# A weight ring of seven buffers instead of six, one weight block fewer resident, and two loads of a step issued at other points of it

## The chip, the cores and the metric

The kernel runs on one core of one Trainium2 chip. The metric is the device time of that core in microseconds, from the first to the last instruction, as the median of several runs; the profile is one more execution, with its own, slightly longer span. The engines are called by their short names: PE is TensorE (matmuls; PEld its weight loads), DVE is VectorE, ACT is ScalarE, POOL is GpSimd, and SP is SyncE, which here only issues transfers.

## The reference

Two branches work on the same input x (2048 rows of 640, bf16) and are mixed row by row with a gate.

```python
# branch A: attention over a sliding window of 256, 32 heads of 20
qkv = x @ wqkv
scores = (q @ k^T) * 20 ** -0.5, masked to 0 <= i - j < 256
a = (softmax(scores) @ v) @ wo

# branch B: 64 segments of 32 rows, one after the other, 32 heads of 192, memory of 8 rows
mem = mem0
for s in range(64):
    h = concat(mem, x[32 * s : 32 * s + 32])          # 40 rows of 640
    q, k, v = h @ Wq, h @ Wk, h @ Wv                  # each to 32 x 192
    scores = (q @ k^T) * 192 ** -0.5                  # rows of the memory see all, others causal
    o = (softmax(scores) @ v) @ Wo                    # back to 40 rows of 640
    mem, out[s] = o[:8], o[8:]

g = sigmoid(sum(x * gate_w))
out = g * a + (1 - g) * b
```

Each step of branch B needs the memory rows that the step before made, so the 64 steps run in order, and each needs all of Wq, Wk, Wv and Wo (4 x 640 x 6144 elements, 31.5 MB in bf16)[...].

## The kernel before

**Stages.** First branch A runs block by block (128 rows each) and writes its gated result to DRAM. Then a "tail" stage works ahead for branch B: the last 8 rows of every segment are multiplied with Wq, Wk and Wv for all segments at once, and the products are stored to the DRAM tensor `xin`, one record for each segment. Then come the 64 steps of branch B. Beside the earlier stages the resident weights are loaded.

**Weights.** Each of the four weights is cut into four groups of heads (g) and each group into tiles (m): five for q, k and v (384 KB each), six for o (320 KB each), 84 blocks in all. The table `STREAMED` (L1079) names for each weight and group the tiles that are not kept: 22 of 84. These are loaded again in every step through a ring, the pool `b_w` with `RING` buffers (L1074), by SP, in the order in which PE uses them. The others are resident: `EARLY` of them (L1075) are loaded during branch A, the rest later. A ring block may be issued when the buffer's last user, a matmul `RING` blocks earlier, is done. In the trace the streamed blocks are `b_w`, the resident ones `w_q`, `w_k`, `w_v`, `w_o` and `hold`, the tail stage's ring blocks `w_ring`.

**One step.** `pe_order` (L630) and the string `STEP` (L636) fix PE's order by hand: `k0 q0 k1 tk0 tq0 q1 s0 tk1 q2 tq1 k2 v0 p0 s1 tq2 q3 k3 pv0 tk2 v1 p1 s2 oa0 ...`. Here q, k, v are projections of a group (L796, five tiles each), tq and tk transposes (L820), s scores (L876), p the transposed probabilities (L930), pv the values (L958 and L965), oa and ob the output projection (L991), m the memory rows for the next step (L1014). The other engines' orders come from a planner, `Sched`: each operation is given an engine, a duration, a latency, the buffers it reads and writes, and operations it must follow (`after`); the planner runs them against a model of the engines and takes on each engine the ready one with the longest chain behind it. PE and SP keep their given orders.

**The loads of a step on POOL.** `tail_qk` (L734) loads 48 KB of stored q and k products for each group (`b_xg`). `load_tail` (L727) loads the 96 KB of stored v products of the step (`b_xv`, one buffer), which the second half of each values operation reads (L965). `load_x` (L720) loads the next segment's 40 KB of x (`b_hT`, two buffers). POOL also stores the step's result (L1027), reads branch A's rows (L1028) and stores the mix (L1037), and copies the tail products into place for the scores (L833, L852, L854). In the kernel before, `load_tail(s)` and `load_x(s + 1)` are entered when the first name of step s comes up (L1046), with no operation that they must follow: they may go as soon as their buffer is free.

**Branch A's first block.** In `branch_A` the load of the second block of x (L106) is issued behind that of the value weights (L105). In the loop over blocks (L323) the score units are interleaved with "fill": projections and other work for neighbouring blocks, handed out in proportion to the units done (L345). For the first block, which has four units, all of the fill is handed out by the last unit; after it comes the last masking (`cut`) and then the values (L297).

## Time and profile before

| | |
|---|---|
| time, median of 3 runs | 2000.54 us (2000.38 to 2003.24) |
| span of the profiled execution | 2011.8 us |
| granted PE clock, mean | 0.997 |
| step of branch B, mean of 63 | 24.66 us (23.6 to 26.7) |
| bytes moved in all | 618.98 MB |
| of these by SP's queue (weights, mostly) | 563.31 MB |
| blocks streamed in a step | 15 of 384 KB and 7 of 320 KB |

A page of the profile gives busy time by engine, the chain of waits that set the end, and the costliest groups of instructions. A group's line holds the line of the source, the engine, the operation, the tiles written and read, the count, busy time and mean duration, and the idle time before it with what ended it. The view of stretches gives for a window the busy time of each engine with its number of instructions, the granted clock, the mean busy share of the core's 16 DMA engines, and the bytes moved per time; the share can pass 1 a little because consecutive packets overlap. A transfer's landing time runs from its issue to the last of its completions.

### The profile page before, as it was taken

What the parts mean: (1) busy time and instruction counts of PE and PEld (TensorE: products, weight loads), DVE (VectorE), ACT (ScalarE), POOL (GpSimd) and SP (SyncE); (2) the same over time, 40 slices, a digit from 0 to 9 for tenths busy, and PEclk for the clock granted to TensorE, in tenths of its full rate; (3) what the DMA queues carried; (4) which work ended last, traced back from release to release, by engine and by line L of the source; (5) the groups of instructions that cost most, each with busy time, mean ns of one, the idle gap of its engine ahead of it and who ended that gap; (6) DMA issues with size and microseconds to landing.
All of it is one profiled execution on the core that took longest, in us unless ns stands there. A gap on an engine that the chain in (4) does not pass through costs nothing.

```text
span 2011.8 us, 92168 instructions
## 1 busy us (share of the span) xinstructions
PE 1901.9 (95%) x39590; PEld 1400.1 (70%) x39590; DVE 1012.7 (50%) x3338; ACT 950.0 (47%) x1951; POOL 721.9 (36%) x2015
## 2 busy tenths in 40 slices
PE   8999999989999999999999999999999999999998
PEld 6888878656666666666666666676666666666665
DVE  5777853334454444444444445444444444444444
ACT  4888832334444444444444444444444444444443
POOL 5111121243344333334333334333333433333332
PEclk9999999999999999999999999999999999999999
DMA  4222159789999999999999999999999999999997
GB/s 156 79 81 80 36 149 325 213 286 350 364 358 359 346 352 355 355 350 355 352 355 355 351 360 366 345 361 353 354 352 351 356 352 349 358 353 356 351 351 278
DMA packets 259632, 618.98 MB, mean 308 GB/s; under 512 B 40552, under 2 KB 59408, under 8 KB 259216
## 3 DMA queue, kind: packets, MB, share of 16 engines
q1 hardware_dynamic: 227264, 563.31, 77.4%
q0 software_dynamic: 31952, 49.71, 8.4%
q8 instruction: 312, 5.11, 1.0%
q14 instruction: 104, 0.85, 0.1%
HBM read 583.49 MB, written 29.37 MB: 305 GB/s over the span
## 4 chain that ended last, share of the span: by engine, by line
PE 71%; DMA 21%; DVE 3%; ACT 2%; issue 2%; POOL 0%; ACTq 0%; POOLq 0%; DVEq 0%
PE ps_o L991 17%; PE ps_v L796 9%; PE ps_k L796 9%; PE ps_q L796 8%; DMA b_w<-in_B_Wq_dram 7%; DMA b_w<-in_B_Wv_dram 5%; DMA b_w<-in_B_Wo_dram 5%; PE t_psum L605 5%; DMA b_w<-in_B_Wk_dram 3%; PE t_psv L623 3%; PE S_ps L876 2%; PE qk_ps L155 2%; PE ps_pv L958 2%; PE tr_q L820 2%; PE tr_k L820 2%; PE s_ps L251 2%
## 5 line engine op out<-in xcount | busy, mean ns | idle before, releaser
L796 PEld LDWEIGHTS <-b_hT 128*32 128x32 bf16 x15360 | 372.3, 96 | 251.2 <-issue 52.7
L991 PEld LDWEIGHTS <-b_OT 128*64 128x64 bf16 x6144 | 364.2, 110 | 40.9 <-issue 14.9
L796 PE MATMUL ps_k<-w_k,b_hT 128*32 128x384 bf16 x4352 | 234.1, 327 | 3.8 <-issue 0.7
L991 PE MATMUL ps_o<-hold,b_OT 128*64 128x320 bf16 x2560 | 236.0, 301 | 0.9 <-issue 0.9
L942 DVE TENSOR_TENSOR b_PTm<-PT_ps,marks 128x320 bf16<-128x320 f32 x256 | 125.9, 492 | 195.2 <-PE PT_ps L930 195.2
L796 PE MATMUL ps_q<-w_q,b_hT 128*32 128x384 bf16 x3584 | 223.4, 327 | 0.1
L847 DVE TENSOR_TENSOR b_Kz<-tr_k,marks 128x256 bf16<-128x256 bf16 x256 | 108.2, 423 | 215.3 <-PE tr_k L820 210.1
L796 PE MATMUL ps_v<-w_v,b_hT 128*32 128x384 bf16 x3584 | 213.7, 328 | 2.1 <-issue 2.0
L991 PE MATMUL ps_o<-b_w,b_OT 128*64 128x320 bf16 x1792 | 205.5, 300 | 8.2 <-DMA b_w<-in_B_Wo_dram 7.2
L254 ACT ACTIVATE pt<-s_ps 128x1024 bf16<-128x1024 f32 x180 | 183.3, 1026 | 47.8 <-PE s_ps L251 46.2
L969 ACT CAST b_OT<-ps_pv 128x480 bf16<-128x480 f32 x256 | 143.1, 559 | 129.0 <-PE ps_pv L965 129.0
L807 ACT CAST b_tok<-ps_k 128x384 bf16<-128x384 f32 x256 | 122.7, 479 | 166.6 <-PE ps_k L796 158.4
L807 ACT CAST b_vtok<-ps_v 128x384 bf16<-128x384 f32 x256 | 122.7, 479 | 134.5 <-PE ps_v L796 133.7
L739 POOL DMA_DIRECT2D b_xg<-xin x256 | 141.8, 554 | 88.7 <-POOL b_QT L833 53.0
L991 PE MATMUL ps_o<-w_o,b_OT 128*64 128x320 bf16 x1792 | 170.0, 300 | 0.8 <-issue 0.8
L807 ACT CAST b_tok<-ps_q 128x384 bf16<-128x384 f32 x256 | 122.9, 480 | 95.5 <-PE ps_q L796 94.5
L829 ACT COPY b_QT<-tr_q 128x384 bf16<-128x384 bf16 x256 | 123.3, 482 | 86.2 <-PE tr_q L820 84.2
L852 POOL COPY b_K<-b_xg 128x64 bf16<-128x64 bf16 x256 | 60.7, 237 | 264.1 <-PE S_ps L876 254.0
L1037 POOL DMA_DIRECT2D out_dram<-b_ga x126 | 62.5, 496 | 243.3 <-DVE b_ga L1032 233.8
L1020 DVE CAST b_hT<-mem_ps 128x16 bf16<-128x16 f32 x126 | 22.5, 179 | 247.4 <-PE mem_ps L1014 244.1
L796 PE MATMUL ps_q<-b_w,b_hT 128*32 128x384 bf16 x1536 | 130.3, 329 | 12.2 <-DMA b_w<-in_B_Wq_dram 11.1
L796 PE MATMUL ps_v<-b_w,b_hT 128*32 128x384 bf16 x1536 | 130.7, 328 | 10.5 <-DMA b_w<-in_B_Wv_dram 9.1
(155 smaller groups left out, 3699.2 us busy)
## 6 DMA issues: line engine op xcount, KB each, us to landing
b_w<-in_B_Wq_dram SPq DMA_DIRECT2D x384, 384.0 KB, 5.7
b_w<-in_B_Wv_dram SPq DMA_DIRECT2D x384, 384.0 KB, 5.3
b_w<-in_B_Wo_dram SPq DMA_DIRECT2D x448, 320.0 KB, 5.4
b_w<-in_B_Wk_dram SPq DMA_DIRECT2D x192, 384.0 KB, 5.3
xin<-hold POOLq DMA_DIRECT2D x8, 1536.0 KB, 12.4
b_xg<-xin POOLq DMA_DIRECT2D x256, 48.0 KB, 5.0
w_k<-in_B_Wk_dram SPq DMA_DIRECT2D x17, 384.0 KB, 3.7
b_xv<-xin POOLq DMA_DIRECT2D x64, 96.0 KB, 5.2
```

What stands on the lines that cost most here:

```text
L254: nc.scalar.activation(out=pt, in_=sp[:], func=ACT.Exp, scale=scale)
L605: self.nc.tensor.matmul(pt[:, bb, :], lhsT=w[kt][:, c:c + P], rhs=self.xTb[:, kt, t0:t0 + hs * MEM], start=(kt == 0), stop=(kt == KT - 1))
L739: sc.op("POOL", 540, 5000, lambda: nc.gpsimd.dma_start(tile_of(b)[:].rearrange("p i b t -> p (i b t)"), xin[s, :, c:c + 192]), writes=[b])
L796: nc.tensor.matmul(t[32 * j:32 * j + 32, 0:384], lhsT=tile_of(hT)[:, kt, :], rhs=w[:, j * 384:(j + 1) * 384], start=(kt == 0), stop=(kt == ...
L807: nc.scalar.copy(dst, src)
L820: nc.tensor.transpose(t[64 * a:64 * a + 64, k, :], tok["tile"][:, c:c + 64], ident[:], tile_position=(0, 64 * a))
L829: nc.scalar.copy(dst, tq["tile"][:].rearrange("p b (j t) -> p b j t", t=SEG))
L847: nc.vector.tensor_tensor(out=tile_of(Kz)[:, :, :, 0:SEG], in0=src, in1=mk_z.unsqueeze(1).unsqueeze(3).to_broadcast([P, 4, 2, SEG]), op=AL ...
L942: nc.vector.tensor_tensor(out=tile_of(PTm)[:], in0=src.to_broadcast([P, 2, 4, L]), in1=mk_m.unsqueeze(1).unsqueeze(3).to_broadcast([P, 2, ...
L969: sc.op("ACT", 560, 50, lambda: nc.scalar.copy(tile_of(OT)[:, 0:12 * L], o["tile"][:, 0:12 * L]), reads=[o], writes=[OT])
L991: nc.tensor.matmul(t[64 * h:64 * h + 64, 0:D // 2], lhsT=OT["tile"][:, c:c + 64], rhs=w, start=(g == 0 and m == 0 and n == 0), stop=(g == ...
L1037: sc.op(eng, 500, 3000, lambda h=h: queue.dma_start(half(outf, h), mine(tile_of(ga), h)), reads=[ga])
```

## The change

It has four parts.

- The ring has seven buffers instead of six. One more block is streamed in each step, tile 2 of group 2 of k, and with it 23 of 84 are; one fewer is loaded early (23 instead of 24), so that the space in SBUF stays the same.
- `load_tail(s)` is entered when the first scores operation (s0) of step s comes up, and must follow the operation entered just before, which is ACT's evacuation of q1.
- `load_x(s + 1)` is entered when the first p0 of step s comes up, and must follow ACT's evacuation of v0.
- In branch A the second block of x is loaded ahead of the value weights; and for the first block the fill is handed out more slowly, with the remainder after the last masking and ahead of the values.

```diff
@@ branch_A
             add_qk(1, KT - 1)
+            load_x(1)
             nc.sync.dma_start(wv_sb[:, :, 0:D], wq3[:, :, 2 * D:3 * D])
-            load_x(1)
...
-                while fill and spent * total < (i + 1) * time:
+                while fill and spent * (total + 2 * (nk == 1)) < (i + 1) * time:
                     w, f = fill.pop(0)
...
                 if cut is not None:
                     cut()
                     cut = None
+                for _, f in fill:
+                    f()
                 for r in ready:
@@ branch_B
-    def load_x(s):
+    def load_x(s, after=()):
...
-        return hb, sc.op("POOL", 540, 5000, f, writes=[hb])
+        return hb, sc.op("POOL", 540, 5000, f, writes=[hb], after=after)
-    def load_tail(s):
+    def load_tail(s, after=()):
...
-        if s not in tails:
-            tails[s] = load_tail(s)
-            if s + 1 < nseg:
-                hts[s + 1] = load_x(s + 1)
+        if n[0] == "s" and s not in tails:
+            tails[s] = load_tail(s, [sc.ops[-1]])
+        if n[0] == "p" and s + 1 < nseg and s + 1 not in hts:
+            hts[s + 1] = load_x(s + 1, [sc.ops[-1]])
@@ the tables
-RING = 6
-EARLY = 24
+RING = 7
+EARLY = 23
...
-            "k": ((1,), (4,), (), (4,)),
+            "k": ((1,), (4,), (2,), (4,)),
```

## The prediction

> **What bounds the kernel now.** I read the chain of waits first, then the busy tenths and the transfers, then stretches of the trace. The page gives the span and the chain by engine:

> ```profile
> span 2011.8 us, 92168 instructions
> PE 71%; DMA 21%; DVE 3%; ACT 2%; issue 2%; POOL 0%; ACTq 0%; POOLq 0%; DVEq 0%
> ```

> The end is set by TensorE with weight transfers threaded in; DVE, ACT and POOL (50%, 47%, 36% busy) are nowhere on it for long. The 64 recurrent steps take most of it: the memory matmuls of L1014 first start at 451.1 and last at about 2004.4 us, so 63 step periods of 24.66 us. Three stretches, with the columns PE, PEld, DVE, ACT, POOL busy, clock, DMA share, GB/s: an early one with resident loads alone, the steps, and two moments inside one step:

> ```profile
> 302.00:308.00 6.00, 6.00 (x58) 5.37 (x56) 1.88 (x6) 1.94 (x6) 2.29 (x2) 1.00 1.03 404
> 452.00:2004.00 1552.00, 1471.04 (x33128) 1055.17 (x33120) 746.13 (x2707) 695.39 (x1575) 602.45 (x1753) 1.00 0.98 353
> 996.00:1001.00 5.00, 5.00 (x130) 2.99 (x126) 2.81 (x10) 2.91 (x7) 2.09 (x7) 1.00 1.03 403
> 1004.00:1007.00 3.00, 3.00 (x81) 2.05 (x75) 2.12 (x9) 1.81 (x5) 1.76 (x5) 1.00 0.91 303
> ```

> The reader is to see that a DMA share of 0.98 isn't a full DMA: the same engines move 404 GB/s with a deep queue, 353 on average in the steps, and swing between 403 and 303 inside one step. Why the queue isn't deep shows in issue-to-landing times (minimum, median, maximum): first single resident loads of the k weights between 50 and 220 us, with nothing beside them; then the burst of resident v loads (285 to 330 us); then the ring's blocks:

> ```profile
> DMA to landing us min/median/max: 3.0/3.1/4.3
> ...
> DMA to landing us min/median/max: 9.2/12.0/14.7
> ...
> DMA to landing us min/median/max: 3.6/5.5/11.8
> ```

> SyncE's own waits are mostly for TensorE to give a ring buffer back (the longest of them first), and after them TensorE's waits, in the steps only (us, times, longest):

> ```profile
> SPq L538 <- PE ps_q L796: 224.6, 312, 1.3
> ```

> ```profile
> PE mem_ps L1014 <- ACT b_OT L1000: 35.6, 62, 0.6
> PE ps_q L796 <- DMA b_w<-in_B_Wq_dram: 10.9, 20, 1.4
> PE ps_o L991 <- DMA b_w<-in_B_Wo_dram: 7.0, 12, 1.3
> ```

> With 22 blocks in 24.66 us and 5.5 us to land, 22 x 5.5 / 24.66 = 4.9 of the six buffers are in flight and 1.1 hold data that is waited on or read. So TensorE and the ring drive each other in a loop. The listed DMA waits are only some 30 us, but short ones hide under the modelled matmul ends. Reading each of the 22 first uses in the trace, and taking the distance to the use before it only where the block had landed 0.25 us or more ahead (70% of them), the medians add up to 23.59 us. So TensorE alone would make a step in 23.6 us, and about 1.06 us of each step, 67 us in all, is late weights.

> [...] a share of about 1.0 goes with 303 to 404 GB/s. [...] the highest stretch here is 404. [...] POOL's 96 KB tail load takes a median 5.2 us to land, like a 384 KB block.

> **The change, part by part.**

> *One more streamed block (k, group 2, tile 2).* Adds one issue of 0.33 us on SyncE, which has room (23 x 0.33 = 7.6 us per step), and 393 KB per step: 353 GB/s x 24.66 us = 8.70 MB becomes 9.10 MB, +4.5%. If the rate stayed at 353, a step would take 25.78 us, +1.12, or +70 us over 63 steps. TensorE's work is the same. Its first use falls in k2, between the second q2 block and v0, where no block is used for 1.7 us today: the demand gets more even.

> *A ring of seven.* No instruction; each block may be issued one block earlier. In flight goes from 4.9 to 5.9 if holding stays at 1.1. The rate for 5.9 isn't in the trace. I bound it: from below, 353, nothing gained (the stalls are then not from short queues); from above, 388 GB/s, which is 9.10 MB in TensorE's 23.6 us and lies under the 404 shown. In between, a saturating curve 404 x (1 - e^(-n/2.37)) is put through 353 at n = 4.9; it gives 139 for one load in flight, where the single load has 393 KB / 3.1 us = 127, so it is fair; at 5.9 it gives 371. The curve thus recovers a third of the 51 GB/s lost; the upper end two thirds. The even demand and the next point speak for more than the curve, so I take 45%: 376 GB/s, 24.20 us, -0.46 per step, -29 us.

> *Tail values and next inputs later.* Same two POOL issues (0.54 us each) and bytes per step. Now they go out together near 20.5 and 21.9 us after a step's start, next to the result's stores, where the trace's rates are among the lowest (308 to 335 GB/s in my reading of 53 steps folded together; 377 to 399 at 2 to 6 us). In the changed program, POOL's order has the tail load after the first output store and ahead of the copies for K, and the input load after a query copy and ahead of a b_xg load. The input has a step to land: nothing. The copies behind the tail load come 0.54 us later, but s1 uses them about 2 us after they end today: nothing. The b_xg load moved by 0.54 us lands as its copy becomes free to run, and that again is ahead of its scores by some 2 us: nothing.

> The tail load itself gets a new wait. It now waits for ACT's cast of q1, and the first values matmul needs it:

> ```profile
> 998.58 0.48 ACT L807 CAST b_tok<-ps_q 128x384 bf16<-128x384 f32 x1 [0.51 <-PE ps_q L796]
> 998.79 0.50 POOL L1037 DMA_DIRECT2D out_dram<-b_ga  x1 [3.67 <-DVE b_ga L1032]
> 1004.54 0.21 PEld L965 LDWEIGHTS <-b_xv 128*64 128x64 bf16 x6
> ```

> The store ends at 999.29 us, so the load goes out there, 5.3 us ahead of its use (median 5.4 over 54 steps). Its landings today: median 5.2, 5% to 95% from 4.4 to 6.6. Setting every landing against every margin, 41% come late, 0.27 us in the mean: +17 us over 63 steps. Behind it on TensorE queue the turning of K and v1's matmuls, which everything follows, so it counts, unless a late weight would have stopped TensorE there anyway. Bounds: 0, if late weights cover it, and +76, if every landing took the 6.6 us of the slowest twentieth (1.2 us x 63). I take 17.

> *Prologue.* The second x load goes ahead of the 800 KB value weights; today the second turning waits 0.57 us for ACT, not for it: 0. The first block's fill is spread out and its remainder moved after the last masking, where TensorE stands 2.17 us for DVE today (L297 at 27.12 us): -2, between 0 and -3. Then one resident load fewer and one ring load more ahead of the steps, beside matmuls: 0.

> *Sum against the 2011.8 us span:* -29 + 17 - 2 = -14, so 1998. The timed runs lie 11 us below the profiled one, median 2000.5: 1986.

> **Rivals.**

> *A, slower: the DMA can't give more.* Place: the 16 engines in the steps; mechanism: the slow stretches come from POOL's small transfers and scattered stalls, not from a short queue, and a seventh buffer only lengthens the queue. For it: share 0.98, stretches of 303 with several blocks outstanding. Against: 404 with the deep queue, beside POOL stores too. Price: at 363 GB/s 25.07 us, +0.41, +26 us, with tail wait and prologue +41: 2041; at 353, 2085. It decides once the rate stays below 372 GB/s, where the gain equals the tail wait and the prologue's 2 us (24.66 - 0.24 us).

> *B, no change: the tail wait takes the late weight's place.* The ring gains hardly more than on the curve (372 to 373 GB/s: 24.46 to 24.40 us, -12 to -16 us) and the tail wait and the prologue, +15, take it back: about 2000. For it: the margin of 5.4 us against 5.2. Against: TensorE's stop lets the ring fill, so that the next late weight is shorter.

> *C, faster than forecast:* the waits for weights vanish and TensorE is the bound at 23.6: -67 with the tail wait partly inside and the prologue, about 1945. For it: 388 is under 404. Against: it needs two thirds of the loss back for one buffer.

> That the change doesn't do what it says is excluded: its order of instructions has the moved loads and the extra block.

> **How the numbers follow.** Forecast (1965 to 1996): 0.42. A: 0.36. B: 0.09. C: 0.13. Measurement can't tell a change under about 0.2%, 4 us. Faster 0.42 + 0.13 = 0.55, same 0.09, slower 0.36. The predicted time is the forecast's 1986. The range for eight in ten goes from C's 1945 to A's 2040, leaving out A's saturated end and the extreme of C.

> **What would show it.** Right: 23 blocks per step, GB/s in the steps near 376, period near 24.2 us, landing of ring blocks still under 6 us with fewer waits of L796 and L991 for DMA, a new wait of L965 for b_xv of 10 to 20 us in total, and no 2.17 us stop before L297. Wrong: landing near 6.5 us with the rate below 370 and as many waits for weights as before (A), or a wait for b_xv far over 20 us.

## The result and the profile after

The changed kernel takes 2022.49 us in the median (2015.53 to 2027.65), beside 2000.46 us (1995.45 to 2003.24) for the kernel before. The ratio is 1.0111, with a 95% interval of 1.0073 to 1.0148: slower by about 22 us, where 14 us faster was forecast.

The profiled spans differ by only 7 us (2011.8 and 2018.8), because the profiled execution of before lay 11 us above its own timed median, and the one of after did not. That matters below: part of the loss seen in the profile of before belonged to that execution.

The page of after, span and chain of waits by engine:

```profile
span 2018.8 us, 92233 instructions
PE 78%; DMA 12%; DVE 4%; issue 3%; ACT 3%; POOL 0%; SPq 0%; ACTq 0%; POOLq 0%; DVEq 0%
```

The chain holds less DMA than before (12% against 21%), yet the kernel is slower. The same stretches as before (columns PE, PEld, DVE, ACT, POOL busy, clock, DMA share, GB/s):

```profile
302.00:308.00 6.00, 6.00 (x57) 5.38 (x55) 1.74 (x5) 1.97 (x6) 1.31 (x1) 1.00 1.04 393
452.00:2004.00 1552.00, 1462.99 (x32918) 1041.33 (x32920) 736.54 (x2696) 694.31 (x1566) 601.75 (x1754) 1.00 1.01 368
```

The share of 1.04 means packets that overlap in the records: in the first stretch 16.5 are open at once in the mean, on the 16 engines that the page counts. In the steps the rate rose from 353 to 368 GB/s, but each step now carries 4.5% more bytes, and 368 / 353 is only 4.2% more. The ring blocks' landing (minimum, median, maximum) moved from 5.5 to 5.8 us in the median:

```profile
DMA to landing us min/median/max: 3.4/5.8/10.7
```

SyncE's longest wait for a ring buffer, and the first of TensorE's waits, in the steps (us, times, longest):

```profile
SPq L540 <- PE ps_q L798: 213.2, 244, 2.3
```

```profile
PE mem_ps L1016 <- ACT b_OT L1002: 36.5, 63, 0.9
PE ps_o L993 <- issue: 9.4, 12, 1.4
PE ps_v L798 <- DMA b_w<-in_B_Wv_dram: 7.4, 13, 1.7
PE S_ps L878 <- issue: 5.0, 8, 1.5
PE ps_pv L967 <- DMA b_xv<-xin: 4.9, 8, 1.2
PE ps_o L993 <- DMA b_w<-in_B_Wo_dram: 4.8, 6, 1.3
```

(Lines of before are two lower: L796 is L798 here.) Waits for q's weights, the longest before, have left the top. What came in their place is the tail values (b_xv) and "issue": a stop that nothing visible ended. The tail load's path in one step:

```profile
1001.62 0.50 POOL L1039 DMA_DIRECT2D out_dram<-b_ga  x1 [3.68 <-DVE b_ga L1034]
1002.11 0.57 POOL L731 DMA_DIRECT2D b_xv<-xin  x1
1007.37 0.21 PEld L967 LDWEIGHTS <-b_xv 128*64 128x64 bf16 x6
```

The load is issued right behind the store, 5.3 us ahead of its use, as the prediction had it. The first memory matmul starts at 447.4 us, where it was 451.1; the mean step is 24.83 us, where it was 24.66.

### A ledger of the step, and what "issue" is

For every streamed block whose landing time is on record (seven in eight are), I took the distance from the first use of the block before to its own first use, in 54 steps, and subtracted the tenth percentile of that same distance. Where the block landed under 0.1 us ahead of its use or later, the excess is a *late weight*; an excess over 0.1 us with the block already there is an *other stall*. The last column adds up TensorE's "issue" waits between 460 and 1980 us.

| kernel | blocks, buffers | step, us | late weights, us per step | other stalls, us per step | "issue" waits, us |
|---|---|---|---|---|---|
| before | 22, 6 | 24.66 | 0.75 | 0.23 | 10.0 |
| prologue alone (same steps as before) | 22, 6 | 24.45 | 0.40 | 0.32 | 10.7 |
| seven buffers, no extra block | 22, 7 | 24.26 | 0.05 | 0.61 | 22.5 |
| ring pair | 23, 7 | 24.53 | 0.10 | 0.70 | 29.5 |
| extra block, six buffers | 23, 6 | 25.07 | 1.09 | 0.20 | 8.4 |
| both moves | 22, 6 | 24.69 | 0.41 | 0.55 | 16.2 |
| after | 23, 7 | 24.83 | 0.38 | 0.63 | 25.0 |
| 13 streamed | 13, 6 | 23.59 | 0.00 | 0.03 | 0.0 |
| 13 streamed, both moves | 13, 6 | 23.58 | 0.00 | 0.01 | 0.6 |

The step is the mean of all 63. The blocks without a landing time are in neither column; their excess over 0.1 us is 0.00 to 0.21 us per step (0.12 before, 0.21 after). The second row runs the same steps as the first and is the better base: its profile lies where its timed runs do.

The other stalls are mostly the "issue" waits. One of them, of the ring pair alone, in the order of time (start us, us, engine, line, operation; in brackets the idle time before it and what ended it):

```profile
493.87 0.56 ACT L969 CAST b_OT<-ps_pv 128x480 bf16<-128x480 f32 x1 [0.55 <-PE ps_pv L965]
...
495.12 0.19 PE L876 MATMUL S_ps<-b_Kz,b_QT 128*64 128x40 bf16 x1
...
496.81 0.46 PE L991 MATMUL ps_o<-w_o,b_OT 128*64 128x320 bf16 x4 [1.51 <-issue]
```

TensorE stands from 495.3 to 496.81 us. The weight w_o is resident, b_OT was ready at 494.43: no operand is missing. What is in the transfers' records at that moment is a packet of 16,384 bytes on queue 8, from 494.53 to 495.52, 1.29 us before the matmul starts. The page of after has that queue, and TensorE's instructions:

```profile
PE 1901.9 (94%) x39590; PEld 1391.9 (69%) x39590; DVE 1006.9 (50%) x3338; ACT 952.7 (47%) x1951; POOL 720.7 (36%) x2015
...
q8 instruction: 312, 5.11, 1.0%
```

In the seven kernels of the table that have such waits in number there are 203 of them, and they end in a narrow band after the end of such a packet: 1.17 to 1.63 us, median 1.43. Of random moments 17% lie within 1 us of a packet's end, of these waits none. The place in the program tells more. When one of these waits ends, the number of instructions that the trace has recorded of TensorE so far (weight loads, matmuls and semaphore instructions) leaves 193 when divided by 256: the same remainder for all 203, so that each wait stands at the same point of a run of 256 instructions. My reading is that TensorE was waiting for its own instructions. With 22 or 23 blocks streamed, these waits took 8.4 to 29.5 us in the steps of the kernels of the table.

### The profile page after: what moved, and what is told of

Read it like the earlier page. It is cut to its first block, busy times and chain, and to the rows that moved or that the text cites. A ratio compares the mean times of both kernels' runs of the same rounds, so it can differ in the third digit from the quotient of the medians.

```text
span 2018.8 us, 92233 instructions
## 1 busy us (share of the span) xinstructions
PE 1901.9 (94%) x39590; PEld 1391.9 (69%) x39590; DVE 1006.9 (50%) x3338; ACT 952.7 (47%) x1951; POOL 720.7 (36%) x2015
## 3 DMA queue, kind: packets, MB, share of 16 engines
q8 instruction: 312, 5.11, 1.0%
## 4 chain that ended last, share of the span: by engine, by line
PE 78%; DMA 12%; DVE 4%; issue 3%; ACT 3%; POOL 0%; SPq 0%; ACTq 0%; POOLq 0%; DVEq 0%
PE ps_o L993 20%; PE ps_v L798 10%; PE ps_k L798 9%; PE ps_q L798 9%; DMA b_w<-in_B_Wv_dram 4%; PE t_psum L607 4%; DMA b_xv<-xin 3%; PE S_ps L878 3%; PE t_psv L625 3%; PE qk_ps L155 2%; PE ps_pv L960 2%; PE tr_k L822 2%; PE tr_q L822 2%; PE s_ps L251 2%; PE PT_ps L930 2%
## 5 line engine op out<-in xcount | busy, mean ns | idle before, releaser
L798 PEld LDWEIGHTS <-b_hT 128*32 128x32 bf16 x15360 | 369.0, 96 | 233.1 <-issue 35.5
L798 PE MATMUL ps_k<-w_k,b_hT 128*32 128x384 bf16 x4096 | 233.7, 327 | 3.1 <-DVE b_hT L783 0.3
L798 PE MATMUL ps_q<-w_q,b_hT 128*32 128x384 bf16 x3584 | 224.8, 328 | 1.9 <-issue 1.9
L798 PE MATMUL ps_v<-w_v,b_hT 128*32 128x384 bf16 x3584 | 214.7, 328 | 2.0 <-issue 1.9
L1029 POOL DMA_DIRECT2D b_dram<-b_OT x128 | 64.1, 506 | 371.3 <-ACT b_OT L1002 371.3
L895 ACT ACTIVATE S_ps<-S_ps 128x160 f32<-128x160 f32 x256 | 74.5, 291 | 150.4 <-DVE S_ps L892 139.5
L798 PE MATMUL ps_v<-b_w,b_hT 128*32 128x384 bf16 x1536 | 133.5, 328 | 10.4 <-DMA b_w<-in_B_Wv_dram 7.4
L1022 DVE CAST b_hT<-mem_ps 128x16 bf16<-128x16 f32 x126 | 22.5, 178 | 241.4 <-PE mem_ps L1016 238.1
```

The costliest lines, as they stand in the source:

```text
L798: nc.tensor.matmul(t[32 * j:32 * j + 32, 0:384], lhsT=tile_of(hT)[:, kt, :], rhs=w[:, j * 384:(j + 1) * 384], start=(kt == 0), stop=(kt == ...
L895: nc.scalar.activation(out=view(), in_=view(), func=ACT.Exp, scale=scale)
```

## The experiments

Ratios are to the kernel before, on the same chip, with 95% intervals.

### The ring pair alone

```diff
-RING = 6
-EARLY = 24
+RING = 7
+EARLY = 23
...
-            "k": ((1,), (4,), (), (4,)),
+            "k": ((1,), (4,), (2,), (4,)),
```

> The kernel before with the ring pair alone (seven buffers, the k block streamed, one resident block fewer). Theory L (the moved loads lose): the seventh buffer pays for the block, about 2000 us, within 6 us of before. Rival R (the ring pair loses): the rate of the transfers doesn't rise enough, 2015 to 2025 us.

2008.4 us, 1.0037 (1.0023 to 1.0051), 372 GB/s in the steps, step 24.53 us. The part that was to bring 29 us costs 7, between what the two theories said. TensorE's waits in the steps, the long memory wait aside:

```profile
PE ps_o L991 <- issue: 6.5, 6, 1.5
PE ps_q L796 <- issue: 6.0, 10, 1.5
PE S_ps L876 <- issue: 4.9, 6, 1.1
PE ps_v L796 <- issue: 4.5, 10, 1.0
```

Not one wait for a weight is among the first four. The ring did its work on the late weights, and the time went elsewhere.

### Both moved loads alone

```diff
...
-        if s not in tails:
-            tails[s] = load_tail(s)
-            if s + 1 < nseg:
-                hts[s + 1] = load_x(s + 1)
+        if n[0] == "s" and s not in tails:
+            tails[s] = load_tail(s, [sc.ops[-1]])
+        if n[0] == "p" and s + 1 < nseg and s + 1 not in hts:
+            hts[s + 1] = load_x(s + 1, [sc.ops[-1]])
```

> The kernel before with the two moved loads alone, ring of six. Theory L: the tail load comes late at the first values matmul and the small transfers gather where the weights are needed most: 2015 to 2025 us. Rival R: the moves cost nothing, within 6 us of before.

2015.1 us, 1.0061 (1.0046 to 1.0076): the moves cost 12 to 14 us, and nothing of this needs the seventh buffer.

### The prologue alone

```diff
+            load_x(1)
             nc.sync.dma_start(wv_sb[:, :, 0:D], wq3[:, :, 2 * D:3 * D])
-            load_x(1)
...
-                while fill and spent * total < (i + 1) * time:
+                while fill and spent * (total + 2 * (nk == 1)) < (i + 1) * time:
...
+                for _, f in fill:
+                    f()
```

> The kernel before with the two edits in branch A alone. Both theories: 2 to 4 us less than before, since the first memory matmul came 3.7 us sooner in the changed kernel's trace.

1996.48 us, 0.9971 (0.9959 to 0.9983): 5 to 6 us gained. This kernel beats both.

### Seven buffers without the extra block

```diff
         self.tiles[u] = t
+        if u == ("k", 2, 1):
+            self.tiles["k", 2, 2] = t
...
-RING = 6
-EARLY = 24
+RING = 7
+EARLY = 23
...
+    allp.remove(("k", 2, 2))
```

> The kernel before with seven buffers and 22 streamed blocks: the k block of group 2, tile 2 is neither streamed nor loaded; its matmuls read tile 1's data, so that part of k is computed from other weights. It measures the seventh buffer by itself. Theory L: the short queue is what holds the transfers back, 1945 to 1970 us. Rival R (the transfer engines are full): within 8 us of before.

1990.36 us, 0.9944 (0.993 to 0.9958). The seventh buffer is worth 11 us with the bytes unchanged, more than the rival theory's 8 and far less than the 30 or more of theory L, and the extra block costs 18 us on top (2008.4 - 1990.36). TensorE's waits show why it isn't worth more:

```profile
PE ps_v L798 <- issue: 6.7, 10, 1.6
PE S_ps L878 <- issue: 4.5, 5, 1.6
PE ps_q L798 <- issue: 4.4, 8, 0.9
PE tr_k L822 <- issue: 2.8, 3, 1.3
...
PE ps_q L798 <- DMA b_w<-in_B_Wq_dram: 1.1, 4, 0.5
```

Against the prologue-only kernel, the better base, late weights fall from 0.40 to 0.05 us per step, but other stalls rise from 0.32 to 0.61. With what is in neither column, the loss falls from 0.93 to 0.71 us, as the step does from 24.45 to 24.26.

### Each moved load alone

The tail values at s0 with the next inputs where they were:

```diff
...
-        if s not in tails:
-            tails[s] = load_tail(s)
-            if s + 1 < nseg:
-                hts[s + 1] = load_x(s + 1)
+        if n[0] == "s" and s not in tails:
+            tails[s] = load_tail(s, [sc.ops[-1]])
+        if s + 1 < nseg and s + 1 not in hts:
+            hts[s + 1] = load_x(s + 1)
```

> The kernel before with the tail load alone moved, ring of six. Theory W (the loss of the moved loads is TensorE's new wait for the tail values): nearly all of the two moves' 12 us, so 2010 to 2014 us. Rival G (it is the gathering of small transfers at 5 to 12 us of a step): about half, 2004 to 2008 us.

2006.25 us, 1.002 (1.0 to 1.0039). The next inputs at p0, with the tail values where they were:

```diff
...
         if s not in tails:
             tails[s] = load_tail(s)
-            if s + 1 < nseg:
-                hts[s + 1] = load_x(s + 1)
+        if n[0] == "p" and s + 1 < nseg and s + 1 not in hts:
+            hts[s + 1] = load_x(s + 1, [sc.ops[-1]])
```

> The kernel before with the next input's load alone moved. Theory W: no change, within 3 us of before, since the input has most of a step to land. Rival G: 4 to 8 us slower.

2005.05 us, 1.0016 (1.0001 to 1.0032). Both medians lie where the theory of gathered transfers put them, or just short of it. The load that was costed at nothing seems to cost as much as the one that TensorE waits for, though both are at the edge of what can be told. Together they make 0.36%, which with its uncertainty reaches to the 0.61% of the pair.

### The extra block with six buffers

```diff
-EARLY = 24
+EARLY = 23
...
-            "k": ((1,), (4,), (), (4,)),
+            "k": ((1,), (4,), (2,), (4,)),
```

> The kernel before with 23 streamed blocks and still six buffers; the freed buffer's space stays empty. It measures the block's price by itself. Transfers held back by a short queue: more than the 18 us that the block cost with seven buffers (2008 against 1990), 2030 to 2050 us. Transfer engines full, one rate whatever the queue: 2065 to 2072 us.

2044.56 us, 1.0229 (1.02 to 1.0259). With six buffers the block costs 43 us by the medians (2002.04 for the kernel before there) and 46 by the ratio, with seven 18. The waits are for weights again:

```profile
PE ps_q L796 <- DMA b_w<-in_B_Wq_dram: 11.9, 27, 1.2
PE ps_k L796 <- DMA b_w<-in_B_Wk_dram: 8.8, 21, 0.8
PE ps_v L796 <- DMA b_w<-in_B_Wv_dram: 8.2, 17, 1.1
PE ps_o L991 <- issue: 3.6, 6, 1.0
```

So the two kinds of stall stand in for each other: late weights 1.09 and other stalls 0.20 us per step here, 0.10 and 0.70 with the seventh buffer. That a stop for a weight gives the next instructions time to arrive is what I make of it; the table shows the exchange, not the reason. A part of the reason is in the traces, and stands with the kernel of thirteen blocks below: with seven buffers the fetches start later.

### The tail values at the same place, but a step ahead

Two buffers for the tail values, so that the load at s0 of step s brings those of step s + 1, and TensorE can't wait for them.

```diff
...
-"xv": (1, [P, 384])
+"xv": (2, [P, 384])
...
+        if 0 not in tails:
+            tails[0] = load_tail(0)
+        if n[0] == "s" and s + 1 < nseg and s + 1 not in tails:
+            tails[s + 1] = load_tail(s + 1, [sc.ops[-1]])
...
```

> As the tail load moved alone, at the same place of the step, but for the step after, into two buffers; the place is made by not loading the k block of group 2, tile 2, whose matmuls read tile 1's data instead, so that part of k is computed from other weights. The traffic is that of the moved load, its wait is gone. Theory W: back to before, 1998 to 2004 us. Rival G: as slow as with the tail load moved alone.

2005.54 us, 1.0024 (1.0009 to 1.0038). The wait is gone, but the time is that of the tail load moved with its wait (1.002): the wait itself is worth -6 to +4 us, taking the two intervals together. So the transfer costs at that place by itself, without TensorE stopping for it.

### Thirteen blocks streamed

```diff
+        for other, same in SAME_AS.items():
+            if u == same:
+                self.tiles[other] = t
...
+SAME_AS = {('q', 2, 4): ('q', 2, 0), ('q', 3, 3): ('q', 3, 1), ('q', 1, 3): ('q', 1, 0), ...}
...
+    allp = [u for u in allp if u not in SAME_AS]
```

> The kernel before with 13 streamed blocks a step instead of 22, ring of six: nine blocks of q, k and v are neither streamed nor loaded, and their matmuls read the data of a resident tile of the same group, so that those parts are computed from other weights. Theory F (TensorE's waits that nothing visible ends are its own instructions, whose fetches the weight traffic delays): with the transfers at some 60% they go, from 10 us in the steps of the kernel before to under 3, and a step falls to TensorE's 23.5 us: 1935 to 1945 us. Rival N (they have nothing to do with the traffic): 8 us or more of them stay, and a step stays above 23.6 us.

1942.15 us, 0.9702 (0.9664 to 0.974). The stretch of the steps:

```profile
452.00:1900.00 1448.00, 1408.93 (x32326) 1017.66 (x32326) 727.43 (x2645) 683.56 (x1539) 592.09 (x1722) 1.00 0.72 220
```

and all that the view of TensorE's waits lists between 460 and 1980 us:

```profile
PE mem_ps L1017 <- ACT b_OT L1003: 36.5, 63, 0.9
PE S_ps L879 <- POOL b_QT L836: 1.0, 1, 1.0
```

With the transfers at a share of 0.72, every "issue" wait has gone (10.0 us before), although TensorE runs through its instructions faster than in any kernel with more traffic, and fetches as many packets (260 in the 63 steps, of 0.96 us in the median; 260 of 1.02 us in the ring pair). So it is the weight traffic, at a share of 0.98 before, that makes stalls of them.

A packet takes hardly longer in the full kernel (1.02 us beside 0.96), but it starts later. The trace has no time of its request; what it does show is how many recorded instructions TensorE has left, when a packet starts, to the next of the points at which the waits stand. The median is 215 here, 147 to 153 in the four kernels of the table with six buffers and 22 or 23 blocks, and 134 to 136 in the three with seven. With six buffers and 23 blocks it is 149, with seven buffers and 22 blocks 136: what the seventh buffer adds to the delay goes with the depth of the ring and not with its bytes. That the fetch stands behind more weights in a queue is a reading; no run shows the queue itself.

The step, 23.59 us, is the figure that the prediction had worked out for TensorE alone.

### The changed kernel again, and without its moves

> The changed kernel once more, beside its parts. If the parts add up (1.0037, 1.0061 and 0.9971 multiplied): a ratio of 1.007, 2015 us. If seven buffers make the moved loads dearer: the 1.011 of the first measurement, 2022 us or more.

2021.65 us, 1.0092 (1.0063 to 1.0121), nearer to the first measurement than to the sum of the parts, though its interval holds both 1.007 and 1.011.

The second kernel is the changed one with both loads back where they were:

```diff
-        if n[0] == "s" and s not in tails:
-            tails[s] = load_tail(s, [sc.ops[-1]])
-        if n[0] == "p" and s + 1 < nseg and s + 1 not in hts:
-            hts[s + 1] = load_x(s + 1, [sc.ops[-1]])
+        if s not in tails:
+            tails[s] = load_tail(s)
+            if s + 1 < nseg:
+                hts[s + 1] = load_x(s + 1)
```

> The changed kernel with both loads back where they were. If the parts add up: 1.0037 x 0.9971 = 1.0008, within 5 us of before. If the moved loads aren't what separates the changed kernel from before: 2010 us or more.

2005.85 us, 1.0016 (0.9996 to 1.0037). The moves cost 16 us with seven buffers, beside 12 to 14 with six: within what can be told, the parts add up. 1.0037 x 1.0061 x 0.9971 is 1.0069, within the interval of the second measurement of the changed kernel and just under that of the first; that the moves are a few us dearer with seven buffers isn't excluded.

### Both moves, with thirteen blocks streamed

The edit of "Both moved loads alone", on top of the kernel with 13 blocks:

```diff
...
+        if n[0] == "s" and s not in tails:
+            tails[s] = load_tail(s, [sc.ops[-1]])
+        if n[0] == "p" and s + 1 < nseg and s + 1 not in hts:
+            hts[s + 1] = load_x(s + 1, [sc.ops[-1]])
```

> Thirteen blocks streamed in a step, six buffers (nine streamed tiles read a neighbouring tile's data and are not loaded, as in e9_13_streamed, so the output is computed with other weights), and both moved loads (tail values at s0, next inputs at p0). With the loads where they were, this kernel took 1942 us, 0.970 of the time before, with steps of 23.59 us and no wait of TensorE that nothing visible ends. Theory F (the moved loads cost because they fall on full transfer engines, and TensorE's instructions are fetched through the same engines): with the engines at 0.72 nothing is held up, so the step stays within 0.1 us of 23.59, time 1938 to 1948 us, and tail values land in under 5 us. Rival theory W (the moved loads cost by their place: the tail wait, and POOL's work behind them): the margin of 5.3 us is as short as before and POOL's order the same, so the cost of 12 us stays: step 23.75 to 23.8, time 1951 to 1957 us, ratio 0.975 to 0.978.

1944.03 us, 0.9709 (0.9672 to 0.9745), step 23.58 us beside 23.59. With the transfers at a share of 0.73 (220 GB/s) the moves don't lengthen the step. The tail load's landing there (minimum, median, maximum):

```profile
DMA to landing us min/median/max: 2.9/3.2/4.9
```

It was 5.2 us in the median in the changed kernel. So the cost of the moves lies in what they share with the weights. The records show that they do share: in the steps of after 15.8 packets of SP's queue are open in the mean where none of POOL's is, 14.9 beside one of POOL's, 14.0 beside two and 12.0 beside four. Which of the two ways it takes (a weight held up, or a fetch) isn't settled: with both moves at six buffers other stalls rise from 0.32 to 0.55 us per step, of which 0.09 are waits for the tail values; from the ring pair to the changed kernel it is the late weights that rise, from 0.10 to 0.38.

## Why the prediction was wrong

**What bounds the kernel: right in kind, incomplete.** TensorE alone makes the step in 23.6 us: shown, 23.59. That all of the remaining 1.06 us was late weights was wrong. It was 0.75 in that execution and 0.40 in another with the same steps; 0.23 to 0.32 was other stalls, mostly "issue" waits. These stood in the trace of before (16 of them, 10.0 us), and I passed them over:

```profile
PE ps_v L796 <- issue: 2.9, 5, 1.1
PE S_ps L876 <- issue: 2.9, 3, 1.7
PE ps_o L991 <- issue: 2.0, 3, 0.9
```

Two readings of the stretches were loose, too: the 303 GB/s went with a DMA share of 0.91, not with one of about 1.0, and 404 is the highest of the stretches shown, not of the trace, which has 412 GB/s between 997.10 and 998.30 us.

**A ring of seven: the step that failed.** The saturating curve gave 371 GB/s for the pair. I raised this to 376, "45%" of the way, since "the even demand and the next point speak for more than the curve". The pair ran at 372, and its step, 24.53 us for 9.10 MB, is 371 GB/s: the curve's number was right, the addition wrong. That the number was right is partly luck. It was the curve's value for 5.9 blocks in flight, and the pair had 23 x 5.8 / 24.53 = 5.4, because more of its buffers held data (1.6 instead of 1.1); for 5.4 the same curve gives 363. (The upper bound had a slip: 9.10 MB in 23.6 us is 386 GB/s, not 388.) And 371 is the pair's break-even: with the step of the prologue-only kernel, the rate at which 23 blocks take no longer than 22 is 9.10 MB / 24.45 us = 372 GB/s. With the profiled step of before, from an execution 11 us above its timed median, it comes out at 369 (9.10 / 24.66), so that the forecast also started from too much loss to recover. Instead of -29 us the pair gave +7: the seventh buffer -11 with 22 blocks, the block +18 on top. The mechanism was half right. The buffer did remove nearly all late weights (0.40 to 0.05 us per step), as rival C had wanted; but TensorE did not come down to 23.6, because other stalls took the place (0.70 us per step, mostly waits that I read as waits for its instructions). No rival had this. Rival A had the right sign and a nearby price (2041), but its reason, that a seventh buffer only lengthens the queue while weights stay late, is not what the trace shows. A deeper ring has its part in the other stalls all the same: with seven buffers the fetches start later, as the counts of 134 to 136 instructions beside 147 to 153 show. How it delays them was not shown.

**The extra block.** Costed at 1.12 us per step if the rate stayed. With six buffers it cost 43 to 46 us, 0.68 to 0.73 per step, as the rate rose to 364 GB/s by itself. So holding the rate still, as that step did to start with, overstated the price of this block.

**Tail values: the wait is there, but half as long, and it isn't what costs.** In the changed kernel the groups that read the tail values sat idle for them as follows (us, times); the two lines below part this into weight loads and matmuls:

```profile
  DMA b_xv<-xin: 12.7, 21
...
  PEld L967: 7.8, 13
  PE ps_pv L967: 4.9, 8
```

The 12.7 us count a stop twice where both wait: the 8 of the matmuls are among the 13 of the weight loads. So TensorE stood 7.8 us in 13 of 63 steps, where 17 us and 41% of the steps were forecast. And taking the wait away gave nothing back that could be told (-6 to +4 us), while the load moved alone cost 4 us (0 to 8). That fits rival B's idea that such a wait takes the place of another; the cost is in where the 96 KB travel.

**Next inputs: "nothing" was most likely wrong.** The step argued only from when the data are needed. The load alone costs 0.16% (3 us; 0.01 to 0.32%), and both moves together lose 12 to 16 us, a loss that was seen with the transfers at a share of 0.99 to 1.01 and not at 0.73. So a transfer with a whole step to land need not be free where it takes the place of weight packets that are just in time.

**Prologue: right in sign, too small.** -2 was forecast, the run gave -5 to -6 (-3 to -8 by its interval), and the first memory matmul of the changed kernel came 3.7 us earlier. Which of the two edits brought how much wasn't run. The stop before L297 shrank as forecast, from 2.17 us to this (us, times, longest):

```profile
PE o_ps L297 <- DVE pt L257: 0.3, 1, 0.3
```

**The sum.** -29 + 17 - 2 was forecast; +7, +12 to 16 and -6 were measured in the parts, so +13 to +17, where the whole gave +19 to +22; the intervals of the parts are wide enough for the rest. The ring pair's term alone was off by 36 us, as much as the whole forecast; the other terms were off by a few us each.

## What to carry to other kernels

When a loop is bound by TensorE and a weight stream that nearly fills the transfers (a share of 0.98 to 1.01 here), list TensorE's "issue" stops beside its waits for data: a deeper ring removed late weights (0.40 to 0.05 us per step), but the program itself is among the transfers (4.1 packets in a step here, each in the place of one of another queue), and of what was run here only less traffic removed both. A ring buffer that is paid for with one more streamed block has to beat that block's bytes, and here it did not; take the break-even from the timed runs and not from one profiled execution. When a small load is moved, ask which transfers it meets there, and not only when its data are needed.

## What the runs showed of the hardware

The queue that the page calls "instruction" and that I take to bring TensorE's program (255.9 recorded instructions of TensorE to a packet of 16,384 bytes in the steps of after) took 1.0% of the 16 engines' span (5.11 MB of 644 MB), and yet TensorE had 22.5 to 29.5 us of "issue" waits with seven buffers; it started again 1.43 us (median) after the end of such a packet. All 203 of these waits stood at one point of every 256 instructions. With the transfers at a share of 0.72 to 0.73 there was no such wait in one kernel, with as many packets (260), and 0.6 us in another. Beside more traffic the packets took about as long (1.02 us in the ring pair, 0.96 with 13 blocks) but started later: with 215 instructions left in the median at 220 GB/s, 147 to 153 at 353 to 364 GB/s with six buffers, 134 to 136 at 359 to 372 with seven. Packets of the three queues took each other's place: 16.2 others open just ahead of a packet of queue 8 and 15.0 beside it; 15.8 of SP's with none of POOL's open and 14.0 with two. A transfer of 96 KB beside the full weight stream (368 GB/s) landed in a median of 5.2 us, and in 3.2 us beside one of 13 blocks (220 GB/s), with the same issue point.
